# First products of the last two batches: two pairs of token blocks at once

## The chip, the cores and the metric

The kernel runs on one core of one Trainium2 chip. A core has a matrix engine (PE; PEld is its weight load), a vector engine (DVE), a scalar engine (ACT), a general one (POOL, also called GpSimd) and a queue engine that issues most transfers (SP). The metric is the device time of one execution in microseconds. Before the change the median of three runs is 464.58 us (464.53 to 464.72).

## The reference

Four batches of 768 tokens. An attention with a decaying state gives x with 384 columns (8 heads of 48), and a mixer follows:

```python
    for t in range(S):
        state = f[:, :, t, :, None] * state + np.einsum('bhd,bhe->bhde', k[:, :, t], v[:, :, t])
        y[:, :, t] = np.einsum('bhd,bhde->bhe', q[:, :, t], state)
...
    xt = x.transpose(0, 2, 1)
    h = xt @ U @ V
    u = x + h.transpose(0, 2, 1)
    ch = np.maximum(u @ w_ch1, 0.0) @ w_ch2
    return (u + ch).astype(np.float32)
```

`f` is the sigmoid of `f_logit`. `w_ch1` is 384x1536, `w_ch2` 1536x384; everything is float32.

## The kernel before

**Attention.** There are 16 units (4 batches by 4 pairs of heads). A unit's tokens are cut into 12 chunks; scans on DVE (L936, L954) give the decays, PE makes scores (`sc`, L1035), turns (`pt`), what a chunk adds to the state (`ds`, L1086) and the output (`y`, L1129 and L1147), all products on a part of the array. Between these stand pieces of the mixer of the batch before, as filler for PE.

**Mixer.** x of a batch lies as 6 blocks of 128 tokens. The low-rank part (`ph`, `pu`) is added to x; then pairs of blocks are turned (`put`, L327; copied to `uT` by ACT, L328), so that a batch has 3 pairs. *First products* give z, 1536 hidden columns for each token, and ReLU. For batches 0 and 1 they are plain (`pz`, L339): 128x128 weights by the 256 columns of a pair of blocks. *Second products* multiply z of a pair with w2 in 7 block products instead of 8 (`pw`, L428, 192 columns). For this each pair needs four ready sums S1 to S4 of 128x768 (`sums_of`): S1 = z10 + z11, S2 = S1 − z00, S3 = z00 − z10, S4 = z01 − S2, where z with index r, c is token block r and half c of the hidden columns. S1 and S2 feed products themselves.

**Batches 2 and 3.** Their six pairs (0 to 5) take the first products through `fewer(a)` (`pp`, L536). A pair is 2 token blocks by 3 blocks of x's columns, w1 3 by 3 blocks of 512 columns, and 15 products take the place of 18. They multiply sums of x (10 for each pair, `X_SUMS`, DVE) with sums of w1 (14, made once by `sum_of_w`, L989). Each is done in four column groups of 128x128 weights by 128 columns of x: 60 products for each pair, 360 in all. Two products share a tile of PSUM. `settle` then combines them by a list, `VALUES`: 21 operations of 512 columns on each pair (19 adds on DVE, 2 copies on ACT), and a ReLU by ACT (L526) where one of z's six blocks is complete.

**Order.** The pieces from the last attention steps to the end are not run when they are called but recorded; `ORDER2`, a list written out by hand (243 numbers before), sets the order in which they are issued. Each engine then works through its own instructions in that order and waits by semaphores for what it needs. PSUM has three buffers of two banks (`ps_big`: `pp`, `put`, `pu` and one `pw`) and two of one bank (`ps_mm`: `pz`, `pw` and others). `Fill` gives attention its filler: `kept` holds the second products of batch 1's last pair, which are left for it.

Of the kernel before, what the change touches and what calls it, by code (L numbers as in the profile page):

```python
# [194 lines left out]
class Mixer:  # L195
# [6 lines left out]
    def __init__(self, tc, b, x, U, V, w1, w2, sums, ident, blocks, out, two, three, zp, ps_big, ps_mm, wide=False,  # L202
                 z_all=None, room=None, pair=0, kept=0):
# [129 lines left out]
        def ch1(a, j):  # L333

            pm = ps_mm.tile([P, 512], F32, name="pz", tag="mm")
            for i in range(2):
                for m in range(NDC):
                    o = (2 * j + i) * P
                    nc.tensor.matmul(pm[:, i * 2 * P : (i + 1) * 2 * P], lhsT=w1[:, m, o : o + P],  # L339
                                     rhs=uT[a][:, m, :], start=(m == 0), stop=(m == NDC - 1))  # L340
# [77 lines left out]
        def products(a, parts, *of):  # L418

            if 0 in parts:  # L420
                if (room["last"] == a - pair) if room else (a == NA - 1 - kept):
                    W["pm"] = ps_big.tile([P, 2, 512], F32, name="pw", tag="big")[:, 0]
                else:
                    W["pm"] = ps_mm.tile([P, 512], F32, name="pw", tag="mm")
            for n in parts:
                lhs, rhs = of[n]
                for i in range(NI):
                    nc.tensor.matmul(W["pm"][:, n * HM : (n + 1) * HM], lhsT=lhs[:, i, :], rhs=rhs[:, i, :],  # L428
                                     start=(i == 0), stop=(i == NI - 1))
# [4 lines left out]
        def seven(a, step, parts=(0, 1)):  # L434
            x0, x1 = x_of.get(2 * a, x[:, 2 * a, :]), x_of.get(2 * a + 1, x[:, 2 * a + 1, :])
            last_of_all = b == out.shape[0] - 1 and a == NA - 1
            if step == 0:
# [8 lines left out]
            elif step == 1:  # L446
# [10 lines left out]
            elif step == 2:  # L457
# [3 lines left out]
                add(W["o1"], W["o1"], pm[:, 0:DM], ALU.add)  # L461
                store(2 * a + 1, W["o1"])
                add(W["s"][:, hi], W["s"][:, hi], pm[:, hi], ALU.add)
                if last_of_all:
                    store(2 * a, W["o0"], lo)
# [1302 lines left out]
```

## Time and profile before

| | before |
|---|---|
| median of 3 runs | 464.58 us |
| the profiled execution | 465.49 us |
| its span | 463.8 us |
| busy PE, DVE, ACT, POOL | 454.1, 363.0, 171.9, 49.5 us |
| PE on `pz`, `pw`, `pp` in the chain that ended last | 18%, 27%, 18% of the span |
| granted clock | 0.998 |

The span is the time from the first to the last instruction of the profiled execution. PE is busy to 98% of it; before about 170 us there are short gaps, later hardly any. A product in float32 shows as two instructions of PE.

### The profile page before, as it was taken

The page shows a single profiled execution, that of the slowest core. Times are in us where ns is not written, and L with a number is a line of the kernel's source. Part 1 is how long each engine was busy: PE and PEld are TensorE (multiplying, and loading weights), DVE is VectorE, ACT ScalarE, POOL GpSimd, SP SyncE. Part 2 cuts the span into 40 slices and gives each one's busy share as a digit, 9 for nine tenths or more (in the row PEclk, how much of TensorE's full clock was granted, in tenths as well). Part 3 has the DMA queues.
Part 4 walks back from the last instruction along what each step waited for, and adds up shares of the span by engine and source line. Part 5 has one row for each costly group of instructions (what it writes and reads, how often), then busy time and mean ns, then how long its engine had stood idle before and what let it go on. Part 6 is the DMA issues. An engine that isn't in the chain of part 4 may idle for free.

```text
span 463.8 us, 13155 instructions
## 1 busy us (share of the span) xinstructions
PE 454.1 (98%) x5687; PEld 394.9 (85%) x5687; DVE 363.0 (78%) x614; ACT 171.9 (37%) x325; POOL 49.5 (11%) x58
## 2 busy tenths in 40 slices
PE   8999999999999999999999999999999999999997
PEld 5876888876666578899988889999989999999996
DVE  6668688988999689677799895879797974878652
ACT  6765776644332135234413542241212311212200
POOL 2002345544110101011000000000000000000000
PEclk9999999999999999999999999999999999999999
DMA  9948997678778814662406100000000100000001
GB/s 193 191 106 211 228 205 175 157 132 111 111 113 120 127 21 55 90 90 28 86 1 112 29 3 11 29 1 1 17 19 1 36 0 18 18 1 35 1 35 40
DMA packets 148584, 34.37 MB, mean 74 GB/s; under 512 B 136934, under 2 KB 146982, under 8 KB 148518
## 3 DMA queue, kind: packets, MB, share of 16 engines
q1 hardware_dynamic: 147718, 33.29, 37.2%
q8 instruction: 47, 0.77, 0.7%
q10 hardware_dynamic: 800, 0.15, 0.2%
q14 instruction: 19, 0.16, 0.1%
HBM read 28.70 MB, written 4.72 MB: 72 GB/s over the span
## 4 chain that ended last, share of the span: by engine, by line
PE 84%; DVE 7%; SPq 2%; ACT 2%; issue 2%; DMA 2%; POOL 0%; DVEq 0%; ACTq 0%; POOLq 0%
PE pw L428 27%; PE pz L339 18%; PE pp L536 18%; PE po L394 5%; PE y L1129 2%; SPq L721 2%; PE sc L1035 2%; PE y L1147 2%; PE ds L1086 2%; PE pt L1062 1%; DVE late L936 1%; PE put L327 1%; PE pt L837 1%; PE pt L895 1%; DMA w<-in_q_dram 1%
## 5 line engine op out<-in xcount | busy, mean ns | idle before, releaser
L339 PE MATMUL pz<-uT,w 128*128 128x256 f32 x420 | 96.4, 383 | 0.1
L339 PEld LDWEIGHTS pz<-uT,w 128*128 128x128 f32 x420 | 77.9, 190 | 10.9 <-ACT uT L328 0.3
L428 PE MATMUL pw<-w,z_all 128*128 128x192 f32 x216 | 37.7, 328 | 0.0
L428 PE MATMUL pw<-zw,w_raw 128*128 128x192 f32 x216 | 37.6, 328 | 0.0
L428 PEld LDWEIGHTS pw<-w,z_all 128*128 128x128 f32 x216 | 35.1, 190 | 0.9 <-DVE qT L243 0.5
L428 PEld LDWEIGHTS pw<-zw,w_raw 128*128 128x128 f32 x216 | 35.2, 190 | 0.5 <-issue 0.3
L116 POOL TENSOR_TENSOR w<-w_y,w_r 128x384 int32<-128x384 int32 x24 | 31.5, 1312 | 36.9 <-DVE w_y L115 22.5
L526 ACT ACTIVATE other<-other 128x512 f32<-128x512 f32 x18 | 11.4, 631 | 44.2 <-DVE other L243 44.2
L526 ACT ACTIVATE z_all<-z_all 128x512 f32<-128x512 f32 x18 | 11.3, 630 | 40.4 <-DVE z_all L243 40.4
L936 DVE TENSOR_TENSOR_SCAN late<-fz,late 128x768 f32<-128x768 f32 x12 | 21.1, 1754 | 6.6 <-ACT fz L931 6.5
L374 ACT ACTIVATE z_all<-pz 128x512 f32<-128x512 f32 x27 | 16.1, 597 | 26.9 <-PE pz L339 26.5
L394 PE MATMUL po<-w,zw 128*128 128x384 f32 x72 | 25.1, 495 | 0.0
L394 PE MATMUL po<-w,z_all 128*128 128x384 f32 x72 | 24.7, 493 | 0.0
L536 PE MATMUL pp<-v_nat,late 128*128 128x128 f32 x168 | 21.6, 276 | 0.0
L394 PEld LDWEIGHTS po<-w,zw 128*128 128x128 f32 x72 | 13.2, 190 | 9.6 <-issue 0.8
L1117 POOL COPY st<-added 128x576 f32<-128x576 f32 x8 | 12.5, 1560 | 81.0 <-DVE added L1111 64.6
L954 DVE TENSOR_TENSOR_SCAN late<-fz,other 128x768 f32<-128x768 f32 x12 | 21.0, 1748 | 0.1
L394 PEld LDWEIGHTS po<-w,z_all 128*128 128x128 f32 x72 | 13.3, 190 | 8.9 <-DVE o L243 0.6
L536 PEld LDWEIGHTS pp<-v_nat,late 128*128 128x128 f32 x168 | 20.2, 192 | 0.1
L1094 ACT COPY added<-ds 48x576 f32<-48x576 f32 (+2 forms) x29 | 17.8, 619 | 5.8 <-PE ds L1086 5.4
L536 PE MATMUL pp<-uT,late 128*128 128x128 f32 x144 | 19.3, 277 | 0.0
L113 DVE TENSOR_SCALAR w_y<-w_y 128x384 f32<-128x384 f32 (+3 forms) x27 | 12.1, 448 | 8.9 <-ACT w_y L106 8.9
(219 smaller groups left out, 908.4 us busy)
## 6 DMA issues: line engine op xcount, KB each, us to landing
w_raw<-in_moe_w_ch_dram SPq DMA_DIRECT2D x18, 384.0 KB, 3.8
out_dram<-o SPq DMA_DIRECT2D x17, 192.0 KB, 1.9
v_nat<-in_v_dram SPq DMA_DIRECT2D x16, 144.0 KB, 3.5
v_nat<-in_v_dram SPq DMA_DIRECT2D x32, 72.0 KB, 3.6
zw<-in_moe_w_ch_dram SPq DMA_DIRECT2D x6, 384.0 KB, 4.5
out_dram<-o SPq DMA_DIRECT2D x14, 96.0 KB, 2.2
w<-in_k_dram SPq DMA_DIRECT2D x4, 288.0 KB, 3.9
w<-in_q_dram SPq DMA_DIRECT2D x4, 288.0 KB, 4.3
```

The source lines that it names most:

```text
L113: nc.vector.tensor_scalar(f, f, SMALLEST, LARGEST, ALU.max, ALU.min)
L116: nc.gpsimd.tensor_tensor(dst.bitcast(I32), shaped(y.bitcast(I32)), shaped(r), ALU.add)
L339: nc.tensor.matmul(pm[:, i * 2 * P : (i + 1) * 2 * P], lhsT=w1[:, m, o : o + P], rhs=uT[a][:, m, :], start=(m == 0), stop=(m == NDC - 1))
L374: nc.scalar.activation(z[a, c][:, k : k + 2, :].rearrange("p i t -> p (i t)"), pm, AF.Relu)
L394: nc.tensor.matmul(pm, lhsT=z[a, i // NI][:, i % NI, s * P : (s + 1) * P], rhs=w2[:, i, :], start=(i == 0), stop=(i == NFC - 1))
L428: nc.tensor.matmul(W["pm"][:, n * HM : (n + 1) * HM], lhsT=lhs[:, i, :], rhs=rhs[:, i, :], start=(i == 0), stop=(i == NI - 1))
L526: nc.scalar.activation(dst, dst, AF.Relu, scale=float(SIGNS[n]))
L536: nc.tensor.matmul(pm[:, i, r * P : (r + 1) * P], lhsT=room["w"](wn)[:, r * P : (r + 1) * P], rhs=x_node(a, xn), start=((xn, wn) == of[0]) ...
L936: nc.vector.tensor_tensor_scan(backwards(X, S - 1, S), backwards(f, S, S), backwards(ends, S - 1, S), 0.0, ALU.mult, ALU.add,)
L954: nc.vector.tensor_tensor_scan(Y, f[:, 0:S], starts, 0.0, ALU.mult, ALU.add)
L1094: nc.scalar.copy(added[r, 1:].rearrange("p (e c s) -> p e c s", c=NBL, s=2)[:, e], ds[r, :, 0 : NBL * D].rearrange("p s (c e) -> p e c s", ...
L1117: nc.gpsimd.tensor_copy(st, states.rearrange(by_e, c=NCH))
```

## The change

The six pairs are taken in three joints of two: 0 and 1, 2 and 3, 4 and 5. `joint(j, of)` replaces `fewer(a)`. A product takes the 256 columns of both pairs at once (block r of either pair, side by side), and the 15 products are gone through twice, once for each half c of z's columns. So there are 180 products of 256 columns, 30 sums of x of 256 columns, and as many operations of 512 columns behind the products as before. For a half to be a run of columns in each of w1's three blocks, w1's blocks of 128 columns are stored in another order (`AT`). `uT` gets four fixed slots in one tile, whose last is also `fz1` of the attention; the sums of x have one set of places, so that those of the next joint are made among the products of the second half. z lies in five thirds that go round, and three sums of w1 are copied to other places by ACT (`move_w`).

The ready sums are four pieces now (`sum_of`), and for pairs 1 and 3 S1 and S2 are made on GpSimd (`SUMS`), in all four operations of 128x768 there. `KEPT = 13` of 17 kept pieces stay in the attention; the others stand among the first joint's products. `ORDER2` is written anew, with 315 numbers.

Three places show the new order. First, PE from the last attention unit to the first `pp`, with tile names (`sc`, `ds`, `y` as above; `pw_3544`, `pw_3658`, `pw_3732` are the kept second products of batch 1). Before:

```order
L1086 MATMUL ds_3690<-v_nat_3422,kb_3654 48x48 x24
L428 MATMUL pw_3658<-zw_2308,w_raw_3534 128x192 x6
L428 MATMUL pw_3732<-w2_90,z_all_82 128x192 x6
L1035 MATMUL sc_3740<-qT_3552,kz1_131 64x64 x24
L1147 MATMUL y_3665<-v_nat_3301,A_3614 64x48 x24
L1129 MATMUL y_3791<-st_3717,qT_3552 64x48 x22
L428 MATMUL pw_3732<-zw_2306,w_raw_3532 128x192 x6
L536 MATMUL pp_3829<-uT_3205,late_80 128x128 x4
L536 MATMUL pp_3829<-v_nat_3563,late_80 128x128 x4
L1147 MATMUL y_3791<-v_nat_3422,A_3739 64x48 x24
```

and in the change:

```order
L1109 MATMUL ds_3653<-v_nat_3410,kb_3592 48x48 x24
L433 MATMUL pw_3596<-w2_90,z_all_82 128x192 x6
L1058 MATMUL sc_3698<-qT_3518,kz1_131 64x64 x24
L433 MATMUL pw_3724<-zw_2301,w_raw_3548 128x192 x6
L1152 MATMUL y_3731<-st_3682,qT_3518 64x48 x22
L1170 MATMUL y_3628<-v_nat_3074,A_3550 64x48 x24
L1170 MATMUL y_3731<-v_nat_3410,A_3697 64x48 x24
L1024 MATMUL pp_3811<-turns_128,late_80 128x256 x2
L1024 MATMUL pp_3811<-v_nat_3540,late_80 128x256 x2
```

Pieces of `pw` have left the last unit, and all of the last unit's `y` stands ahead of the first `pp`.

Second, PE from the end of joint 0 into the first half of joint 1, in the change (`pp_4045` is the last product of joint 0, the `pp` behind it belong to joint 1; `pw_4068` and `pw_4110` are second products of pair 0, and `w1_89` under `pw_4110` is its S2, which lies in a place of w1):

```order
L1024 MATMUL pp_4034<-v_nat_3544,late_80 128x256 x2
L1024 MATMUL pp_4045<-v_nat_3544,z_all_82 128x256 x2
L433 MATMUL pw_4068<-w2_90,other_81 128x192 x6
L1024 MATMUL pp_4075<-st_3541,late_80 128x256 x2
L1024 MATMUL pp_4075<-v_nat_3540,late_80 128x256 x2
L433 MATMUL pw_4068<-w2_90,z_all_82 128x192 x6
L1024 MATMUL pp_4091<-st_3541,w1_89 128x256 x2
L1024 MATMUL pp_4091<-turns_128,w1_89 128x256 x2
L1024 MATMUL pp_4096<-turns_128,late_80 128x256 x2
L1024 MATMUL pp_4096<-v_nat_3540,late_80 128x256 x2
L433 MATMUL pw_4110<-zw_2301,w1_89 128x192 x6
```

Between the last product of a joint and the first use of S2 stand two parts of `pw` and three pairs of products. Before, two pairs of blocks did not end together and each pair's sums were made apart.

Third, DVE at the same place. The last add behind `pp_4045`, then the five ready sums that are left to it (S1 of pair 0, S3 of pair 1, S2 of pair 0, S4 of pair 1, S4 of pair 0; S3 of pair 0 was made earlier), and what is queued behind:

```order
L959 TENSOR_TENSOR z_all<-z_all,pp 128x512
L247 TENSOR_TENSOR w_89<-other,z_all 128x768
L247 TENSOR_TENSOR w_raw<-other 128x768
L247 TENSOR_TENSOR w_89<-w_89,other 128x768
L247 TENSOR_TENSOR w_raw<-z_all,w_raw 128x768
L247 TENSOR_TENSOR w_89<-z_all,w_89 128x768
L247 TENSOR_TENSOR w_y<-x,pw 128x192
L247 TENSOR_TENSOR o<-w_y,pw 128x192
L959 TENSOR_TENSOR qT<-kz_131,pp 128x512
```

and POOL's whole list for the joints (S1 and S2 of pair 1, then of pair 3):

```order
L417 TENSOR_TENSOR w_raw<-other,z_all 128x768
L417 TENSOR_TENSOR w_raw<-w_raw,other 128x768
L417 TENSOR_TENSOR w_raw<-other,z_all 128x768
L417 TENSOR_TENSOR w_raw<-w_raw,z_all 128x768
L1767 TENSOR_LOAD ok
```

POOL's S1 waits for the same ReLU as DVE's S1, and DVE's S4 of pair 1 for POOL's S2.

The diff, cut to its core:

```diff
--- before.py
+++ after.py
 ORDER2 = (
-    1, 6, 0, 2, 3, 4, 47, 5, 8, 9, 10, 7, 11, 12, 13, 15, 14, 16, 18, 20, 17, 19, 21, 22, 61, 23, 26, 25, 27, 28,
...
+    10, 1, 2, 0, 3, 4, 5, 6, 8, 7, 9, 11, 12, 13, 14, 15, 16, 17, 18, 19, 20, 21, 22, 23, 25, 26, 27, 24, 28, 29,
...
-            uT[a] = three.tile([P, NDC, 2 * P], F32, name="uT")
+            uT[a] = three.tile([P, NDC, 2 * P], F32, name="uT") if uT_all is None else uT_all(b, a)
...
-                o = (2 * j + i) * P
+                o = at[2 * j + i] * P
...
-            return z[a, c][:, :, r * P : (r + 1) * P]
-
-        def sums_of(a):
-            for i in range(1, 5):
-                if room and a >= pair and (a - pair) % 2 == 0:
-                    s = room["S"][i - 1]
-                else:
-                    s = two.tile([P, WP], U64, name="w_raw", bufs=RAW).bitcast(F32)
-                S[a, i] = s.rearrange("p (i t) -> p i t", t=P)
-            add(S[a, 1], part(a, 1, 0), part(a, 1, 1), ALU.add)
-            add(S[a, 2], S[a, 1], part(a, 0, 0), ALU.subtract)
-            add(S[a, 3], part(a, 0, 0), part(a, 1, 0), ALU.subtract)
-            add(S[a, 4], part(a, 0, 1), S[a, 2], ALU.subtract)
+            return placed[a, r, c] if (a, r, c) in placed else z[a, c][:, :, r * P : (r + 1) * P]
+
+        def sum_of(a, i):
+            if room and a >= pair and (a - pair) % 2 == 0:
+                s = room["S"][i - 1]
+            else:
+                s = two.tile([P, WP], U64, name="w_raw", bufs=RAW).bitcast(F32)
+            S[a, i] = s.rearrange("p (i t) -> p i t", t=P)
+            left, right, op = {1: (part(a, 1, 0), part(a, 1, 1), ALU.add), 2: (S.get((a, 1)), part(a, 0, 0), ALU.subtract),
+                               3: (part(a, 0, 0), part(a, 1, 0), ALU.subtract), 4: (part(a, 0, 1), S.get((a, 2)), ALU.subtract)}[i]
+            if room and i in room["sums"](b, a):
+                nc.gpsimd.tensor_tensor(S[a, i], left, right, op)
+            else:
+                add(S[a, i], left, right, op)
...
-        def x_node(a, n):
-            if n < 6:
-                return uT[a][:, n % 3, n // 3 * P : (n // 3 + 1) * P]
-            return sums_x[a][n - 6]
...
-            def two_of(k):
-                if k == 0:
-                    free.extend(room["values"]())
-                    z[a, 0], z[a, 1] = zf[:, 0:NI, :], zf[:, NI:, :]
-                pm = ps_big.tile([P, 2, 512], F32, name="pp", tag="big")
-                for i, of in enumerate(PRODUCTS[k : k + 2]):
-                    for r in range(FG):
-                        for xn, wn in of:
-                            nc.tensor.matmul(
-                                pm[:, i, r * P : (r + 1) * P], lhsT=room["w"](wn)[:, r * P : (r + 1) * P],
-                                rhs=x_node(a, xn), start=((xn, wn) == of[0]), stop=((xn, wn) == of[-1]),
-                            )
-                    have[k + i] = pm[:, i, 0 : FG * P].rearrange("p (i t) -> p i t", t=P)
-                settle()
...
-            return [] if sums is None else [(1, lambda: sums_of(a))]
+            return [] if sums is None else [(1, lambda i=i: sum_of(a, i)) for i in range(1, 5)]
...
-    fz = [const.tile([P, S + 1], F32, name=f"fz{i}") for i in range(2)]
+    turns_of = const.tile([P, 4 * NDC * 2 * P + 1], F32, name="turns")
+    slots = turns_of[:, 0 : 4 * NDC * 2 * P].rearrange("p (n m t) -> p n m t", n=4, m=NDC)
+    fz = [const.tile([P, S + 1], F32, name="fz0"), turns_of[:, 3 * S :]]
+
+    def slot_of(b, a):
+        return slots[:, (a if b < B - 2 else a + (b - B + 2) * NBL // 2) % 4]
...
+    AT = [i % (NFC // 2) // 2 * 4 + 2 * (i // (NFC // 2)) + i % 2 for i in range(NFC)]
...
+            some = []
+            for i in range(3):
+                some.append(three.tile([P, NBL, 2, D], F32, name="v_nat").rearrange("p c h d -> p (c h d)"))
+                if i < 2:
+                    some.append(two.tile([P, NCH, D], F32, name="st").rearrange("p c d -> p (c d)"))
+            x_places.extend(t[:, i * 2 * P : (i + 1) * 2 * P].rearrange("p (s t) -> p s t", t=P) for t in some for i in range(2))
...
+    NI = NFC // 2
+    thirds = [t[:, i * NI : (i + 1) * NI, :] for t, n in ((of_other, 2), (z_all, 3)) for i in range(n)]
+    room["sums"] = lambda b, a: [(), (1, 2), (3,), (3, 4)][SUMS[(b - B + 2) * NBL // 2 + a]]
+    SUMS = 0, 1, 0, 1, 0, 0
+
+    def move_w(i):
+        t = late.rearrange("p a s -> p (a s)")[:, (4, 7)[i] * FG : ((4, 7)[i] + 1) * FG] if i < 2 else one.tile([P, 2, NBL, PAD], F32, name="kb").rearrange("p h c d -> p (h c d)")[:, 0:FG]
+        nc.scalar.copy(t, w_places[13 + i])
+        w_places[13 + i] = t
...
+    of_z = {}
+
+    def joint(j, of):
+
+        uT = slots[:, j % 2 * 2 : j % 2 * 2 + 2]
+        if j == 0:
+            of_z.update({(0, 0): 0, (0, 1): 1, (1, 0): 2, (1, 1): 3, "free": 4})
+        else:
+            of_z.update({(0, 0): of_z["free"], (1, 0): of_z[0, 0], (1, 1): of_z[1, 0], "free": of_z[1, 1]})
+        z = {cr: thirds[i] for cr, i in of_z.items() if cr != "free"}
+        for s, (m, a) in enumerate(of):
+            for (c, r), t in z.items():
+                m.placed[a, r, c] = t[:, :, s * P : (s + 1) * P]
+
+        def x_node(n):
+            if n < 6:
+                return uT[:, :, n % 3, n // 3 * P : (n // 3 + 1) * P]
+            return places_of_x()[[i for i, *_ in X_SUMS].index(n)]
+
+        def sum_of_x(i):
+            n, p, sign, q = X_SUMS[i]
+            combine(x_node(n), x_node(p), sign, x_node(q))
+
+        def half(c):
...
+            def two_of(k):
+                pm = ps_big.tile([P, 2, 512], F32, name="pp", tag="big")
+                for i, ((xn, wn),) in enumerate(PRODUCTS[k : k + 2]):
+                    for r in range(2):
+                        o = (2 * c + r) * P
+                        nc.tensor.matmul(
+                            pm[:, i, r * 2 * P : (r + 1) * 2 * P].rearrange("p (s t) -> p s t", t=P),
+                            lhsT=w_node(wn)[:, o : o + P], rhs=x_node(xn), start=True, stop=True,
+                        )
+                    have[k + i] = pm[:, i, :].rearrange("p (i t) -> p i t", t=2 * P)
+                settle()
+
+            return [(4 * 2 * P * len(PRODUCTS[k : k + 2]), lambda k=k: two_of(k)) for k in range(0, len(PRODUCTS), 2)]
+
+        return [(1, lambda i=i: sum_of_x(i)) for i in range(len(X_SUMS))], half(0), half(1)
...
+    KEPT = 13
+    attention(pieces, Fill(kept[:KEPT], 33))
...
+    joints = [joint(j, [(mixers[b], a) for b, a in pairs[2 * j : 2 * j + 2]]) for j in range(NP)]
...
+    def mixed(*lists):
+
+        lists, out = [list(t) for t in lists], []
+        while any(lists):
+            out += [t.pop(0) for t in lists if t]
+        return out
+
+    def sums_among(half, j):
+
+        if j >= NP:
+            return half
+        x, out = joints[j][0], []
+        ends = {1: (0, 1, 2), 3: (3, 4), 4: (5, 6), 5: (7,), 7: (8, 9)}
+        for k, p in enumerate(half):
+            out += [p] + [x[i] for i in ends.get(k, ())]
+        return out
+
+    moves = [(1, lambda i=i: move_w(i)) for i in range(3)]
+    x, h0, h1 = joints[0]
+    todo = list(x)
+    todo += mixed(h0, low[:1] + kept[KEPT : KEPT + 1] + low[1:2] + kept[KEPT + 1 : KEPT + 2] + mixers[1].mixes + low[3:4])
+    todo += m.before[-1:] + mixed(sums_among(h1, 1), kept[KEPT + 2 :])
+    todo += moves
+    for j in range(NP):
+        (m0, a0), (m1, a1) = [(mixers[b], a) for b, a in pairs[2 * j : 2 * j + 2]]
+        todo += m0.ready(a0) + m1.ready(a1)
+        A, E = m0.halved(a0), m1.halved(a1)
+        if j + 1 < NP:
+            x, h0, h1 = joints[j + 1]
+            todo += mixed(h0, A)
+            if j == 0:
+                todo += low[4:]
+            todo += E[:2] + mixed(sums_among(h1, j + 2), E[2:])
...
+            todo += A + E
```

More of the change, by code (lines that the diff above doesn't have):

```diff
@@ L202, in __init__ @@
     def __init__(self, tc, b, x, U, V, w1, w2, sums, ident, blocks, out, two, three, zp, ps_big, ps_mm, wide=False,
-                 z_all=None, room=None, pair=0, kept=0):
+                 z_all=None, room=None, pair=0, kept=0, uT_all=None, at=None):
         nc = tc.nc
@@ L440, in seven @@
                     return
-                s = W["s"] = two.tile([P, WP], U32, name="w_y").bitcast(F32)
-                o = W["o0"] = three.tile([P, DM], F32, name="o")
+                s = W[a, "s"] = two.tile([P, WP], U32, name="w_y").bitcast(F32)
+                o = W[a, "o0"] = three.tile([P, DM], F32, name="o")
                 nc.scalar.copy(s[:, hi], pm[:, lo])
@@ L460, in seven @@
                     return
[L461 to L463 removed]
+                add(W[a, "o1"], W[a, "o1"], pm[:, 0:DM], ALU.add)
+                store(2 * a + 1, W[a, "o1"])
+                add(W[a, "s"][:, hi], W[a, "s"][:, hi], pm[:, hi], ALU.add)
                 if last_of_all:
[L465 removed]
+                    store(2 * a, W[a, "o0"], lo)
@@ L545, in second @@
+                add(W[a, "o0"][:, hi], W[a, "s"][:, hi], pm[:, lo], ALU.add)
+                store(2 * a, W[a, "o0"], hi if last_of_all else slice(0, DM))
         def second(a):
@@ L587, in __init__ @@
         self.mixes = [(DM, mix_four), (DM, lambda: [mix(t) for t in range(NG, NCH)])]
-        self.first, self.second, self.ready, self.fewer, self.halved = first, second, ready, fewer, halved
-        self.sums_of_x = lambda a: [(1, lambda: sums_of_x(a))]
+        self.first, self.second, self.ready, self.halved, self.placed = first, second, ready, halved, placed
 def quarters(nc, pool, w2):
@@ new lines, in combine, with place_of, got, settle @@
+    def combine(dst, a, sign, b):
+        nc.vector.tensor_tensor(dst, a, b, ALU.add if sign == "+" else ALU.subtract)
+    of_z = {}
[17 more added lines that the diff above has]
+        def half(c):
+            have, todo, values, uses = {}, list(VALUES), {}, {}
+            for i, v in enumerate(VALUES):
+                for o in (v[1], v[3]):
+                    uses[o] = i
+            def place_of(n):
+                if n < 6:
+                    return z[c, n // 3][:, n % 3 * 2 : n % 3 * 2 + 2, :]
+                if n not in values:
+                    values[n] = places_of_values().pop(0)
+                return values[n].rearrange("p (i t) -> p i t", t=2 * P)
+            def got(o):
+                return have.get(int(o[1:])) if o[0] == "p" else place_of(int(o[1:]))
+            def settle():
+                while todo:
+                    n, p, sign, q = todo[0]
+                    if any(o is not None and got(o) is None for o in (p, q)):
+                        return
+                    todo.pop(0)
+                    i = len(VALUES) - len(todo) - 1
+                    left, right = got(p), None if q is None else got(q)
+                    dst = place_of(n)
+                    if q is None:
+                        nc.scalar.copy(dst, left)
+                    else:
+                        combine(dst, left, sign, right)
+                    for o in (p, q):
+                        if o is not None and o[0] == "v" and int(o[1:]) >= 6 and uses[o] == i and int(o[1:]) != n:
+                            v_places.append(values.pop(int(o[1:])))
+                    if n < 6 and not any(v[0] == n for v in todo):
+                        nc.scalar.activation(dst, dst, AF.Relu, scale=float(SIGNS[n]))
+            def two_of(k):
[11 more added lines that the diff above has]
+        return [(1, lambda i=i: sum_of_x(i)) for i in range(len(X_SUMS))], half(0), half(1)
@@ L1383, in factored_path @@
                     [(t, lambda i=i: sum_of_w(i)) for i, t in enumerate(turns, early_sums)])
-    attention(pieces, Fill(kept[:-1], 33))
+    KEPT = 13
+    attention(pieces, Fill(kept[:KEPT], 33))
     mixers = [m, mixer(B - 1)]
```

104 lines of the change are left out of this document (14 added, 90 removed), and 23 rows, old and new, of the table ORDER2.

## The prediction

> **What bounds the kernel now.** I read the page's busy row first, then the table of windows over the stage that changes, then the chain of waits.
>
> ```profile
> PE 454.1 (98%) x5687; PEld 394.9 (85%) x5687; DVE 363.0 (78%) x614; ACT 171.9 (37%) x325; POOL 49.5 (11%) x58
> ```
> ```profile
> 250.00:290.00 40.00, 40.00 (x816) 35.85 (x818) 31.72 (x53) 17.80 (x30) 0.00 (x0) 1.00 0.14 27
> 375.00:400.00 25.00, 25.00 (x188) 25.00 (x187) 15.36 (x31) 4.54 (x9) 0.00 (x0) 1.00 0.02 9
> 400.00:425.00 25.00, 25.00 (x194) 25.00 (x193) 19.86 (x34) 4.86 (x8) 0.00 (x0) 1.00 0.07 25
> 425.00:450.00 25.00, 25.00 (x178) 25.00 (x178) 17.28 (x30) 4.10 (x7) 0.00 (x0) 1.00 0.05 16
> ```
>
> The columns of a window are its bounds, its length, busy time (and instructions) of PE, PEld, DVE, ACT and POOL, the granted clock, the DMA share and GB/s. From 250 us on PE has no gap and the clock is 1.00; DVE is busy for 61 to 79% and POOL for nothing. A microsecond of PE work taken out of this stage is therefore one off the span as long as DVE keeps up, and every wait that PE is given is one on it. The chain of waits, whose rows are runs of work with start, length and count, has the prices:
>
> ```profile
> 58.31 5.18 PE pz L339 x24
> 69.99 2.59 PE pz L339 x12
> 73.10 2.79 PE pz L339 x12
> 296.50 5.36 PE pp L536 x48
> 311.71 3.77 PE pp L536 x32
> 319.39 3.57 PE pp L536 x32
> 349.17 0.52 PE put L327 x12
> 399.89 1.95 PE pw L428 x12
> 436.93 23.42 PE pw L428 x144
> 460.37 0.35 DVE o L243
> ```
>
> Every float32 product of the program shows as two instructions here. One instruction of 128 columns (pp) takes 5.36/48 = 111.6 ns, of 256 columns (pz) 5.18/24 = 215.8 ns, of 192 columns (pw) 1.95/12 = 162.5 ns. The first run behind a product on a part of the array costs 0.20 us more (3.77 against 3.57, 2.79 against 2.59).
>
> **The change, part by part.** *Products.* 360 products of 128 columns (720 instructions, 80.35 us) become 180 of 256 (360 instructions, 77.69 us): 2.66 us less. The new order has 55 passages from partial to full products where there were 56: 0.20 us less. Together −2.86 us. I price the new pp like pz, since both multiply a 128x128 block of weights by 256 columns of SBUF; the bounds are nothing (256 columns cost two of 128) and this.
>
> [...] The sum goes by the rows.
>
> *Three pieces of second products* (pw, 36 instructions, 5.85 us) leave the attention stage and stand behind the first pp. PE's sum stays; what covers the last attention unit gets thinner. In the window from 250 to 290 us DVE is busy for 31.72 us; with 5.85 us of PE work fewer that is 31.72/34.15 = 93%. It fits, so I take 0; the other bound is a third of the cover lost, 2 us.
>
> *x sums, copies, order of w1's columns.* 60 DVE sums of 128 columns become 30 of 256, and three ACT copies of 512 are new; ACT was under 20% busy in the last three windows. They lie beside PE, so nothing by themselves. What they do to DVE's lag comes next.
>
> *The end of a joint.* There DVE must finish the adds behind the products before the ready sums S1 to S4 (768 columns), and S2 feeds a second product. Prices on DVE, from its timeline (start, length):
>
> ```profile
> 371.56 0.28 DVE L243 TENSOR_TENSOR st<-uT,v_nat 128x128 f32<-128x128 f32 x1
> 371.76 0.68 DVE L243 TENSOR_TENSOR z_all<-qT,kz 128x512 f32<-128x512 f32 x1
> 372.36 0.28 DVE L243 TENSOR_TENSOR st<-uT,v_nat 128x128 f32<-128x128 f32 x1
> 372.56 0.68 DVE L243 TENSOR_TENSOR z_all<-z_all,pp 128x512 f32<-128x512 f32 x1
> 373.16 0.68 DVE L243 TENSOR_TENSOR qT<-pp,qT 128x512 f32<-128x512 f32 x1
> ...
> 396.06 0.96 DVE L243 TENSOR_TENSOR w_raw<-z_all 128x768 f32<-128x768 f32 x1 [0.49 <-ACT z_all L526]
> 397.06 0.96 DVE L243 TENSOR_TENSOR w_raw<-w_raw,z_all 128x768 f32<-128x768 f32 x1
> 397.93 0.95 DVE L243 TENSOR_TENSOR w_raw<-z_all 128x768 f32<-128x768 f32 x1
> ...
> 438.80 0.69 DVE L243 TENSOR_TENSOR z_all<-z_all,pp 128x512 f32<-128x512 f32 x1
> 440.18 0.96 DVE L243 TENSOR_TENSOR w_raw<-z_all 128x768 f32<-128x768 f32 x1 [0.70 <-ACT z_all L526]
> ```
>
> From start to start an add of 512 columns takes 0.60 us (a dependent one some 0.1 more, I use 0.62), a 128-column sum 0.20, so 256 columns about 0.34; a 768-column sum 0.87, or 1.00 ahead of one that needs it; and from the end of the last add through the ReLU to the first ready sum it is 0.70.
>
> Joint 0, second half, counted from the end of the first half's last product. PE: transposes 0.52, parts of pw 2.15 and 1.95, 13 products of 4 x 215.8 ns (11.22): the last product (the row pp_4045 in the excerpt) ends at 15.84. DVE has the first product of pp_3994 at about 8.3; from there it has 16 adds (9.9) and 6 x sums (2.0) without a gap, ends the last add at 20.2, and the ready sums can start at 20.9. PE goes on with pw 1.95, pp 1.73, pw 1.95, pp 1.73, pp 1.73 and wants S2 of the first pair (pw_4110) at 24.93: a slack of 4.0 us. In joint 1 the same count from the end of pp_4240 gives the last product at 22.70, the last add at 25.9, the sums from 26.6, and S2 wanted behind pw, pp, pp, pw (7.36) at 30.05: a slack of 3.5. On DVE alone S2 stands third, behind S1 of its own pair and S3 of the other: 0.87 + 0.96 + 0.96 = 2.8 us. Both fit, by 1.2 and 0.7 us.
>
> But the last ReLU releases POOL too, which makes S1 and then S2 of the other pair of each of these joints, as operations on two SBUF operands. POOL's prices by shape, from the groups of instructions:
>
> ```profile
> L116 POOL TENSOR_TENSOR U<-w_y,w_r 128x192 int32<-128x192 int32 x1 | 0.6, 593 | 29.5 <-DVE w_y L115 29.5
> L116 POOL TENSOR_TENSOR V<-w_y,w_r 128x128 int32<-128x128 int32 x1 | 0.5, 454 | 1.4 <-DVE w_y L115 1.4
> ```
>
> What the two engines do to each other, from the timeline of both:
>
> ```profile
> 64.82 1.75 DVE L936 TENSOR_TENSOR_SCAN late<-fz,late 128x768 f32<-128x768 f32 x1
> 65.05 2.32 POOL L116 TENSOR_TENSOR w<-w_y,w_r 128x384 int32<-128x384 int32 x1 [1.78 <-ACT w_y L106]
> ...
> 68.94 0.95 DVE L862 TENSOR_TENSOR kz<-pt,late 128x768 f32<-128x768 f32 x1
> 69.16 1.00 POOL L116 TENSOR_TENSOR w<-w_y,w_r 128x384 int32<-128x384 int32 x1 [1.79 <-DVE w_y L115]
> ...
> 71.29 1.75 DVE L954 TENSOR_TENSOR_SCAN late<-fz,other 128x768 f32<-128x768 f32 x1
> 71.52 2.31 POOL L116 TENSOR_TENSOR w<-w_y,w_r 128x384 int32<-128x384 int32 x1 [1.35 <-DVE w_y L115]
> 72.96 1.09 DVE L113 TENSOR_SCALAR w_y<-w_y 128x384 f32<-128x384 f32 x1
> ```
> ```profile
> 179.66 1.21 POOL L1117 COPY st<-added 128x576 f32<-128x576 f32 x1 [13.34 <-DVE added L1111]
> 180.43 1.26 DVE L865 TENSOR_TENSOR qT<-qT,late 128x768 f32<-128x768 f32 x1
> ```
>
> Beside a DVE operation with an operand in PSUM (pt, at 68.94) POOL's 384 columns take 1.00 us. Behind a scan with two SBUF operands the same takes 2.3: the scan ends at 66.57 and 73.04, POOL 0.80 later. In the other direction a 768-column DVE operation takes 1.26 instead of 0.95 behind POOL's copy, and the DVE operation that stood ready when the scan of 71.29 ended had to wait for POOL (to 74.05). So they take turns, whole operations at a time. POOL costs (1.00 − 0.454)/256 = 2.13 ns a column; 768 columns hold it for 0.80 + 0.82 = 1.62 us.
>
> Taken in turns S2 stands behind three DVE sums and two POOL sums: 2.8 + 2 x 1.62 = 6.1 us after the ReLU. PE then waits 6.1 − 4.0 = 2.1 us in joint 0 and 6.1 − 3.5 = 2.6 us in joint 1. Later waits there are covered: the buffer that the next but one pp wants (pp_4136) is free 9.9 us after the ReLU, and PE, held back already, comes for it at 11.8. The bounds of this term are 0 and, with a POOL sum at 2.0 us (POOL's 1.00 for 384 columns doubled, its start included), 2 x 0.4 more at each place, 6.3.
>
> [...]
>
> *The tail.* The last joint makes all its sums on DVE; its S2 (pair 4) is ready 5.95 to 6.5 us after the last product, by the same count, and wanted after 5.85 (three parts of pw): 0.1 to 0.7, I take 0.3. Behind it the tail is as before, pw and then the 0.35 us at 460.37 with its store.
>
> *Sum:* −2.86 + 2.1 + 2.6 + 0.3 = +2.1 us, 465.49 to 467.6 for the profiled execution. That one lies 0.91 us over the median and holds 463.8 us of span and 1.7 around it; the change leaves what is around, so the median goes from 464.58 to 466.7.
>
> **The rivals.** *No turns (sums on both engines side by side).* For it: none of the colliding rows above has float32 with two operands on POOL. Against it: all the colliding rows. It gives −2.86 + 0.3: 462.0. *DVE keeps its turn* through its three sums, since they stand back to back in its queue. For it: the next DVE sum is queued when one ends. Against it: 72.96, where the queued DVE operation lost. S2 then comes in time, but S4, which DVE makes next, waits for POOL's S2 at 6.1, and the evacuations behind it release a buffer late: about 0.5 us in joint 0 and 1.0 in joint 1, −1.1 in all: 463.5. *The attention stage runs dry* where the three pieces left: DVE ends it, 2 us on top of the forecast, 468.7, or about 464.0 with no turns. It decides from the point where DVE's 93% becomes 100. *Wide products cost two narrow ones:* the −2.66 is gone, 469.3; only a slower read of the two pairs' separate blocks could do it, and no row shows one.
>
> **How the numbers follow.** Forecast 0.47; no turns 0.25; DVE keeps its turn 0.13; attention dry 0.11; no gain of width 0.04. The 0.2% (0.93 us) that can be told from no change lies at 463.65 and 465.5. The forecast is slower except where slack or POOL's price are off by 1.2 us together (0.08 of its 0.47, same for most of that). No turns is faster but for 0.03; the third case is split between faster and same. Faster 0.32, same 0.16, slower 0.52. Range 461.8 to 468.6: from no turns without the tail's wait to the forecast with POOL near its upper bound.
>
> **What would show it.** Right: POOL's four sums of 128x768 at about twice their time beside a free DVE, or DVE's sums of 768 columns at about 2.5 us, two PE gaps of 2 to 3 us ahead of pw at the ends of joints 0 and 1, released by DVE's sum, and none in the attention stage. The new pp's at 216 ns an instruction. Wrong: PE without gaps there and DVE's sums at 0.95 us beside POOL's; or gaps in the last attention unit; or a pp of 256 columns at 223 ns.

## The result

| | before | the change |
|---|---|---|
| median | 464.53 us (9 runs, 463.59 to 465.59) | 468.22 us (9 runs, 465.83 to 469.22) |
| ratio, 95% interval | | 1.0076 [1.0057, 1.0096] |
| profiled execution, span | 465.49, 463.8 us | 469.22, 467.5 us |
| mean granted clock of that execution | 0.998 | 0.996 |

The change makes the kernel slower by 3.7 us. A second measurement gave 468.88 beside 464.75 us, ratio 1.0082 [1.0054, 1.0110]. The forecast was 466.7 us, slower, in a range of 461.8 to 468.6.

The page's busy row of the change, and the table of windows where the three pieces have left and at the program's start:

```profile
PE 453.5 (97%) x5327; PEld 383.1 (82%) x5327; DVE 364.1 (78%) x580; ACT 173.5 (37%) x328; POOL 60.6 (13%) x62
```
```profile
28.00:32.00 4.00, 4.00 (x67) 3.64 (x61) 1.36 (x1) 2.63 (x6) 0.00 (x0) 0.57 0.02 5
250.00:290.00 40.00, 39.91 (x847) 34.00 (x846) 32.09 (x51) 22.82 (x38) 0.00 (x0) 1.00 0.12 23
```

PE is busy for 0.6 us less than before, not 2.9, though it has 360 instructions fewer, and the span is 3.7 us longer. The view of waits names what PE waits for (engine, line, releaser, then the sum, how often, the longest):

```profile
PE pw L433 <- DVE w L247: 4.1, 3, 2.3
PE y L1170 <- issue: 1.6, 1, 1.6
```

The first row is new. The timeline at the end of joint 0 (start, length; all of DVE and POOL, and of the other engines only the ReLU and PE's pw) shows how it comes about:

```profile
328.46 0.63 ACT L1017 ACTIVATE z_all<-z_all 128x512 f32<-128x512 f32 x1 [0.90 <-DVE z_all L959]
329.12 0.96 DVE L247 TENSOR_TENSOR w<-other,z_all 128x768 f32<-128x768 f32 x1 [0.70 <-ACT z_all L1017]
329.17 2.58 POOL L417 TENSOR_TENSOR w_raw<-other,z_all 128x768 f32<-128x768 f32 x1 [110.65 <-ACT z_all L1017]
330.00 2.57 DVE L247 TENSOR_TENSOR w_raw<-other 128x768 f32<-128x768 f32 x1
331.83 2.41 POOL L417 TENSOR_TENSOR w_raw<-w_raw,other 128x768 f32<-128x768 f32 x1
332.49 2.56 DVE L247 TENSOR_TENSOR w<-w,other 128x768 f32<-128x768 f32 x1
334.97 0.95 DVE L247 TENSOR_TENSOR w_raw<-z_all,w_raw 128x768 f32<-128x768 f32 x1
335.10 2.22 PE L433 MATMUL pw<-zw,w 128*128 128x192 f32 x12 [1.68 <-DVE w L247]
```

S1 of pair 0 (DVE, 0.96), S1 of pair 1 (POOL, to 331.75), S3 (DVE, to 332.57), S2 of pair 1 (POOL, to 334.24), S2 of pair 0 (DVE, to 335.05): one at a time, each of the two DVE operations lengthened by the POOL sum ahead of it. The PE row stands in PE's own timeline: S2 is used 0.05 us after it is there, and PE had been idle for 1.68 us. Joint 1 reads alike (DVE's sums up to S2):

```profile
385.27 0.63 ACT L1017 ACTIVATE z_all<-z_all 128x512 f32<-128x512 f32 x1 [0.90 <-DVE z_all L959]
385.94 0.96 DVE L247 TENSOR_TENSOR w<-other,z_all 128x768 f32<-128x768 f32 x1 [0.70 <-ACT z_all L1017]
385.98 2.59 POOL L417 TENSOR_TENSOR w_raw<-other,z_all 128x768 f32<-128x768 f32 x1 [51.75 <-ACT z_all L1017]
386.81 2.57 DVE L247 TENSOR_TENSOR w_raw<-z_all,other 128x768 f32<-128x768 f32 x1
388.65 2.40 POOL L417 TENSOR_TENSOR w_raw<-w_raw,z_all 128x768 f32<-128x768 f32 x1
389.31 2.55 DVE L247 TENSOR_TENSOR w<-w,z_all 128x768 f32<-128x768 f32 x1
391.91 2.22 PE L433 MATMUL pw<-zw,w 128*128 128x192 f32 x12 [2.25 <-DVE w L247]
```

Rows of the change's chain of waits complete the account:

```profile
50.99 7.97 PE pz L343 x36
335.10 2.22 PE pw L433 x12
337.32 1.73 PE pp L1024 x8
339.05 1.95 PE pw L433 x12
391.91 2.22 PE pw L433 x12
440.38 23.68 PE pw L433 x144
```

and one of the chain before:

```profile
49.69 7.97 PE pz L339 x36
```

The first run of 36 pz starts at 50.99 us. The same run started at 49.69 before, so 1.3 us are lost at the program's start, where PE idles for 1.63 us at 25 us and the granted clock is then 0.57 from 28 to 32 us. The last pw take 23.68 us instead of 23.42, and the pw behind the two gaps take 2.22 instead of 1.95 (in the chain; a timeline shows 2.22 and 2.11, as runs overlap there): a run that starts behind a wait costs 0.27 us more, called a restart below. The sum for the profiled executions: −2.86 (products, passages) + 4.1 (gaps) + 0.8 (three restarts) + 1.3 (start) = +3.3 of the measured 3.7 us.

### The profile page after: what moved, and what is told of

Same layout as the page of the kernel before. It is cut to its first block, busy times and chain, and to the rows that moved or that the text cites. A ratio compares the mean times of both kernels' runs of the same rounds, so it can differ in the third digit from the quotient of the medians.

```text
span 467.5 us, 12433 instructions
## 1 busy us (share of the span) xinstructions
PE 453.5 (97%) x5327; PEld 383.1 (82%) x5327; DVE 364.1 (78%) x580; ACT 173.5 (37%) x328; POOL 60.6 (13%) x62
## 4 chain that ended last, share of the span: by engine, by line
PE 85%; DVE 9%; ACT 2%; issue 1%; DMA 1%; SPq 0%; DVEq 0%; ACTq 0%
PE pw L433 24%; PE pz L343 20%; PE pp L1024 13%; PE po L398 10%; PE sc L1058 3%; PE y L1152 2%; PE y L1170 2%; PE ds L1109 2%; DVE w L247 2%; PE pt L1085 2%; DVE z_all L959 2%; PE pt L832 1%; PE pt L774 1%; DVE w_raw L247 1%; PE put L331 1%
## 5 line engine op out<-in xcount | busy, mean ns | idle before, releaser
L343 PE MATMUL pz<-turns,w 128*128 128x256 f32 x420 | 96.2, 383 | 0.1
L343 PEld LDWEIGHTS pz<-turns,w 128*128 128x128 f32 x420 | 77.9, 190 | 10.9 <-ACT turns L332 0.3
L433 PE MATMUL pw<-w,z_all 128*128 128x192 f32 x252 | 44.3, 328 | 0.0
L433 PEld LDWEIGHTS pw<-w,z_all 128*128 128x128 f32 x252 | 41.5, 190 | 1.0
L417 POOL TENSOR_TENSOR w_raw<-other,z_all 128x768 f32<-128x768 f32 x2 | 5.2, 2584 | 162.4 <-ACT z_all L1017 162.4
L1024 PE MATMUL pp<-v_nat,late 128*128 128x256 f32 x104 | 26.2, 379 | 0.0
L1140 POOL COPY st<-added 128x576 f32<-128x576 f32 x8 | 13.6, 1704 | 81.7 <-DVE added L1134 81.7
L433 PE MATMUL pw<-zw,w 128*128 128x192 f32 x108 | 19.2, 329 | 4.1 <-DVE w L247 4.1
L433 PEld LDWEIGHTS pw<-zw,w 128*128 128x128 f32 x108 | 17.7, 190 | 5.3 <-DVE w L247 5.1
```

Of the source, the lines that this page charges most:

```text
L433: nc.tensor.matmul(W[a, "pm"][:, n * HM : (n + 1) * HM], lhsT=lhs[:, i, :], rhs=rhs[:, i, :], start=(i == 0), stop=(i == NI - 1))
L1024: nc.tensor.matmul(pm[:, i, r * 2 * P : (r + 1) * 2 * P].rearrange("p (s t) -> p s t", t=P), lhsT=w_node(wn)[:, o : o + P], rhs=x_node(xn) ...
L1140: nc.gpsimd.tensor_copy(st, states.rearrange(by_e, c=NCH))
```

## The experiments

The theory was the one of the forecast: at a joint's end POOL's and DVE's sums take turns, and S2 comes late. The first rival was that DVE is late there whoever helps it; the order, the moved pieces and the width of the products stood to be separated from both.

### No sum on POOL

```diff
-    SUMS = 0, 1, 0, 1, 0, 0
+    SUMS = 0, 0, 0, 0, 0, 0
```

> The change, with SUMS all 0: DVE makes the four sums that POOL made; nothing is left out. On DVE S2 of the first pair stays third in line (S1 of either pair ahead of it). Turns theory: DVE's sums go back from 2.49 to 0.96 us, S2 is ready 2.8 us after the ReLU, the PE gaps of 1.7 and 2.2 us ahead of pw and the 0.27 us of restart behind each are gone: 4.4 us faster than the change, about 463.8 us. Rival, DVE is late at a joint's end whoever helps it: two more sums for DVE at each of the two joints (4 x 0.87 us), so no faster than the change, 468 to 471 us.

Measured: 462.66 us (10 runs, 461.76 to 463.40), ratio to the kernel before 0.9939 [0.9915, 0.9963]. The timeline of this kernel at the same place:

```profile
327.79 0.96 DVE L247 TENSOR_TENSOR w<-other,z_all 128x768 f32<-128x768 f32 x1 [0.70 <-ACT z_all L1017]
328.67 0.95 DVE L247 TENSOR_TENSOR w_raw<-other,z_all 128x768 f32<-128x768 f32 x1
329.54 0.95 DVE L247 TENSOR_TENSOR w<-w,other 128x768 f32<-128x768 f32 x1
...
331.92 2.11 PE L433 MATMUL pw<-zw,w 128*128 128x192 f32 x12
```

Seven sums stand in a row (the first three are shown) at 0.87 us from start to start; S2, the third of them, is there at 330.5, and PE comes for it at 331.92 without a wait. With more to do DVE is in time, so the rival falls: it was not too slow, it was held up. This kernel beats both: 2.4 us less than the kernel before on that chip (465.03), and 5.6 and 6.2 us less than the two medians of the change. A gain of at least 5.6 against an expected 4.4 was the first sign that the gaps cost more than their own length.

### One turn in the line instead of two

```diff
-    room["sums"] = lambda b, a: [(), (1, 2), (3,), (3, 4)][SUMS[(b - B + 2) * NBL // 2 + a]]
+    room["sums"] = lambda b, a: [(), (1,), (3,), (3, 4)][SUMS[(b - B + 2) * NBL // 2 + a]]
```

> The change, with only S1 of pairs 1 and 3 on POOL, S2 of these pairs on DVE, where it stands between S1 and S2 of the first pair; nothing is left out. Turns theory: one POOL sum stands in the line instead of two, S2 is ready at 3 x 0.93 + 1.62 = 4.4 us after the ReLU instead of 6.0; gaps of about 0.3 and 0.8 us and their restarts are left, so 2.8 us faster than the change, about 465.4 us. Rival, DVE is late anyway: one more DVE sum a joint, slower than the change, 468 to 470 us.

Measured: 464.26 us (10 runs), ratio to before 0.9977 [0.9956, 0.9998], 1.6 us over the kernel with no sum on POOL. PE's gap in its timeline at joint 0, and then at joint 1:

```profile
332.76 2.22 PE L433 MATMUL pw<-zw,w 128*128 128x192 f32 x12 [0.24 <-DVE w L247]
...
388.14 2.22 PE L433 MATMUL pw<-zw,w 128*128 128x192 f32 x12 [0.83 <-DVE w L247]
```

0.24 and 0.83 us, where 0.3 and 0.8 were expected. DVE is late for another reason than in the change, though, as the timeline of DVE and POOL at joint 0 shows:

```profile
328.22 0.96 DVE L247 TENSOR_TENSOR w<-other,z_all 128x768 f32<-128x768 f32 x1 [0.69 <-ACT z_all L1017]
328.26 2.58 POOL L417 TENSOR_TENSOR w_raw<-other,z_all 128x768 f32<-128x768 f32 x1 [110.65 <-ACT z_all L1017]
330.88 0.96 DVE L247 TENSOR_TENSOR w_raw<-w_raw,other 128x768 f32<-128x768 f32 x1 [1.70 <-POOL w_raw L417]
331.76 0.95 DVE L247 TENSOR_TENSOR w<-w,other 128x768 f32<-128x768 f32 x1
```

DVE's second sum is now S2 of pair 1, which needs the S1 that POOL makes. DVE waits 1.70 us for these data, and S2 of pair 0 stands behind it in DVE's queue. So this kernel shows what one POOL sum in the line costs, but not that the engines take turns. It helps in another way: with DVE idle, POOL's sum ends 1.66 us after DVE's S1 (330.84 after 329.18); in the change, with a DVE sum held up beside it, 1.67 us after (331.75 after 330.08). The held sum did not slow POOL, so the two did not share; one waited.

### POOL's sum away from the joint's end

```diff
-    SUMS = 0, 1, 0, 1, 0, 0
+    SUMS = 0, 2, 0, 2, 0, 0
```

> The change, with S3 of pairs 1 and 3 on POOL in place of S1 and S2; nothing is left out. S3 needs only the first half of z, so POOL can make it in the middle of the second half, far from the line of the joint's end. Turns theory: POOL's sum takes 1.6 to 2.6 us and holds up one or two DVE adds by up to 0.8 us there, which DVE's lag passes on to the ReLU (slack 4.0 and 3.5 against 2.8); gaps of 0 to 0.3 us, so within 0.5 us of the kernel with no sum on POOL, about 463.9 us. Rival, any POOL sum between the joints costs its length: half of what the change lost, about 466 us.

Measured: 462.74 us (12 runs), ratio to before 0.9949 [0.9929, 0.9968]: as with no sum on POOL. DVE and POOL in the timeline around POOL's second S3:

```profile
365.81 0.69 DVE L959 TENSOR_TENSOR qT<-A,kz 128x512 f32<-128x512 f32 x1
365.93 2.25 POOL L417 TENSOR_TENSOR w_raw<-z_all,other 128x768 f32<-128x768 f32 x1 [54.21 <-DVE st L959]
366.41 0.55 DVE L247 TENSOR_TENSOR o<-o,pw 128x384 f32<-128x384 f32 x1
366.88 0.35 DVE L247 TENSOR_TENSOR w_y<-w_y,pw 128x192 f32<-128x192 f32 x1
```

POOL waits for DVE's add of two SBUF operands (to 366.50) and then holds on for 1.68 us; DVE's next two operations, which read pw from PSUM, run beside it at 0.55 and 0.35 us, as in the kernel with no sum on POOL. So it is not a sum on POOL that costs, but one whose turn falls between sums of two SBUF operands that PE waits for. It gained nothing either. Of the DVE operations of these rows and of joint 0 that stood beside a float32 sum on POOL, those with two SBUF operands took turns with it (2.57 and 2.56 us behind it in joint 0 instead of 0.95), and the two with an operand in PSUM kept their 0.55 and 0.35 us.

### The width alone

```diff
-                        nc.tensor.matmul(
-                            pm[:, i, r * 2 * P : (r + 1) * 2 * P].rearrange("p (s t) -> p s t", t=P),
-                            lhsT=w_node(wn)[:, o : o + P], rhs=x_node(xn), start=True, stop=True,
-                        )
+                        for s in range(2):
+                            nc.tensor.matmul(
+                                pm[:, i, (2 * r + s) * P : (2 * r + s + 1) * P],
+                                lhsT=w_node(wn)[:, o : o + P], rhs=x_node(xn)[:, s, :], start=True, stop=True,
+                            )
```

beside `SUMS = 0, 0, 0, 0, 0, 0`.

> As the kernel with no sum on POOL, and each product of 256 columns made as two of 128 with the same weights block; nothing is left out. If width is worth what the rows of pz and pp said, 360 more instructions cost 2.66 us more: 466.4 us, less what the slower PE hides of waits (under 0.3). If width were worth nothing the time stays as with 256 columns.

Measured: 465.18 us (11 runs, 464.00 to 466.50; a twelfth took 473.35 us at a mean clock of 0.982), ratio to before 0.9997 [0.9976, 1.0018]. It is 2.5 us over the same kernel with 256 columns. The expectation's 466.4 stood on a base of 463.8; on the measured base of 462.66 it would have been 465.3. So the width is worth what pz and pp of the kernel before said. Order, moves and places without it come to nothing together: this kernel takes the time of the kernel before, within 0.24%.

### The change once more

> The change once more, unaltered, beside the runs of the kernel before on the same chip. The two PE gaps with their restarts (1.68 + 2.25 + 0.18 us and 3 x 0.27 us) less the 2.86 us of products make +2.1 us; the profiled execution of the change also had a stretch from 28 to 32 us at a granted clock of 0.57, about 1.3 us. If that stretch is not of the change, it comes and goes, and the median lies about 2.1 to 2.5 us over the kernel before, or 4.7 us over the kernel with no sum on POOL (467.2 beside 465.0). If it belongs to the change, it is 3.4 to 3.7 us again.

Measured: 468.88 us (7 runs, 466.33 to 470.96), 4.1 us over before. Neither case of the expectation fits: the slow start is not in this profile, and the loss is there. The table of windows of this execution, and PE's timeline behind joint 1's gap:

```profile
389.00:391.00 2.00, 0.52 (x3) 0.52 (x4) 2.00 (x2) 0.00 (x0) 0.61 (x1) 0.99 0.00 0
391.00:393.00 2.00, 2.00 (x8) 2.00 (x7) 2.00 (x5) 0.00 (x0) 0.00 (x0) 0.50 0.01 4
393.00:395.00 2.00, 2.00 (x8) 1.89 (x8) 2.00 (x5) 0.00 (x0) 0.00 (x0) 0.65 0.00 0
395.00:397.00 2.00, 2.00 (x13) 1.87 (x12) 1.54 (x4) 0.00 (x0) 0.00 (x0) 1.00 0.00 0
```
```profile
390.48 3.77 PE L433 MATMUL pw<-zw,w 128*128 128x192 f32 x12 [2.25 <-DVE w L247]
394.04 1.21 PE L1024 MATMUL pp<-v_nat,fz 128*128 128x256 f32 x4
```

Behind the same gap of 2.25 us the granted clock is 0.50 and 0.65 for 4 us, and 12 pw take 3.77 us where 2.22 stood in the first profile of the change. 4 us at a mean of 0.58 are 1.7 us lost. So the low clock is not of the start alone: here it follows a gap that the change made. On this chip 5 of 7 executions of the change have a mean clock of 0.996 or less, and none of 12 of the kernel before. (One stretch as this, 1.7 us lost of 465, makes a mean of 0.996.) Both measurements of the change together: in 6 of 16 executions the mean clock is over 0.996, and their median is 466.8 us (465.83 to 467.84), 2.1 us over the same kind of execution of the kernel before (464.7); in the other 10 the median is 469.05 us, 2.3 us more.

### A third place with turns

```diff
-    SUMS = 0, 1, 0, 1, 0, 0
+    SUMS = 0, 1, 0, 1, 0, 1
```

> The change, with S1 and S2 of pair 5 on POOL too, as those of pairs 1 and 3; nothing is left out. Turns theory: at the last joint's end S2 of pair 4 has no slack (PE waits 0.18 us there already) and then stands behind two POOL sums more, 2 x 1.62 us: a third PE gap of 3.4 us in place of 0.2, so 3.2 us slower than the change, about 470.5 to 471.5 us. Rival, the gaps come from something else than POOL's sums at a joint's end (DVE's load, the new order): DVE has two sums less there, so the same as the change or up to 0.5 us faster.

Measured: 471.48 us (6 runs), ratio to before 1.0136 [1.0116, 1.0157]; 3.3 us over the first measurement of the change, 2.6 over the second, which was taken on the same chip. PE's gap in the last joint:

```profile
443.17 4.17 PE L433 MATMUL pw<-zw,w 128*128 128x192 f32 x24 [3.40 <-DVE w L247]
```

3.40 us where the change waits for 0.18: 3.22 us more, two POOL sums of 1.61 us. Taking two sums off DVE made it later. In this profile too the clock drops behind joint 1's gap of 2.25 us (0.77, 0.50 and 0.88 in the windows of 2 us from 389 to 395 us); behind the gap of 3.40 us it does not (1.00 from 443 to 451 us).

### The gaps filled, and one gap at a time

In the first of three kernels PE works on in the gaps, to see whether the low clock comes without the pause:

```diff
+            if room and 0 in parts and (a, 2) in S and of[0][0] is S[a, 2]:
+                for _ in range({0: 5, 2: 6}.get((b - 2) * 3 + a, 0)):
+                    nc.tensor.matmul(W[a, "pm"][:, 0:HM], lhsT=w2[:, 0, 0:P], rhs=w2[:, 0, 0:HM], start=True, stop=True)
             for n in parts:
                 lhs, rhs = of[n]
```

> The change, with PE kept at work in the two gaps: 5 and 6 products of 192 columns on weights that are long loaded (1.63 and 1.95 us) stand ahead of the pw that waits; their results are overwritten by that pw, and nothing is left out. PE waits for S2 as before, so the gaps stay in the schedule. Clock theory (a PE gap of 1.7 to 2.3 us is at times followed by some 3.5 us at half the granted clock, 1.8 us lost and more): no such stretch behind the joints any more, and no restart of 0.27 us, so the executions lie where those of the change without a stretch lie, 465.8 to 466.5 us, against 468.9 for the median of the change on the same kind of run. Rival, the low clock comes with the program's start or the chip and not with the gaps: 468 to 469 us as the change.

Measured: 467.49 us (13 runs, 466.29 to 470.12), ratio to before 1.0039 [1.0014, 1.0064]. A low mean clock is left in 1 of 13 executions (0.993, 470.12 us). That one is the profiled one. There PE's clock is 1.00 behind both joints, and the first of two slow stretches stands near the program's start, again behind a gap of 1.6 us:

```profile
PE y L1173 <- issue: 1.6, 1, 1.6
```
```profile
28.00:30.00 2.00, 2.00 (x12) 2.00 (x11) 1.24 (x1) 1.21 (x4) 0.00 (x0) 0.55 0.06 18
30.00:32.00 2.00, 2.00 (x53) 1.70 (x52) 0.12 (x1) 1.19 (x2) 0.00 (x0) 0.60 0.00 0
34.00:40.00 6.00, 5.37 (x200) 4.26 (x201) 4.76 (x12) 4.44 (x14) 1.05 (x2) 1.00 0.58 162
40.00:100.00 60.00, 59.54 (x502) 49.74 (x503) 50.98 (x91) 38.23 (x76) 27.96 (x22) 0.97 0.82 190
336.00:340.00 4.00, 3.98 (x22) 3.78 (x23) 3.93 (x7) 0.00 (x0) 0.00 (x0) 1.00 0.00 0
392.00:394.00 2.00, 1.69 (x11) 1.39 (x10) 2.00 (x3) 0.00 (x0) 0.00 (x0) 1.00 0.02 4
394.00:396.00 2.00, 2.00 (x13) 1.87 (x12) 2.00 (x5) 0.00 (x0) 0.00 (x0) 1.00 0.00 0
```

The second lies between 40 and 100 us, where a mean clock of 0.97 is 1.8 us lost. PE is idle for 0.63 us from 34 to 40 us and for 0.46 us in those 60, 1.09 us in all, less than the one gap of 1.6 us ahead of the first: a pause as long as that is not always what comes before a drop. That the low clock is gone behind the joints, and with it most of the slow executions, bears the clock theory out, although the median is 1 us above the band expected. Against the 466.8 us of the change's own undisturbed clock it is 0.6 to 0.7 us, and what that is made of stays open. In this profile PE still waits for 0.32 us behind the fill of joint 1 and the pw behind both fills still take 2.22 us.

The other two have the turns in one joint only:

```diff
-    SUMS = 0, 1, 0, 1, 0, 0
+    SUMS = 0, 0, 0, 1, 0, 0
```

> The change, with S1 and S2 on POOL for pair 3 only, so that joint 1 alone has the turns; nothing is left out. Turns theory: one PE gap of 2.25 us and its restart of 0.27 us, so 2.5 us over the kernel with no sum on POOL, 465.2 us where the clock stays at 1.00, and two more where it drops behind the gap; median 465 to 467.3 us, the mean clock 1.00 in the one kind and 0.996 in the other. Rival, both joints' turns are needed for the loss: as with no sum on POOL, 462.7 us.

Measured: 466.16 us (12 runs), ratio to before 1.0021 [0.9989, 1.0054]. The 7 executions at full clock have a median of 465.2 us, as expected. In 5 of 12 the mean clock is 0.996 or less (466.1 to 471.4 us), and the table of windows of the profiled one shows it behind the gap of 2.25 us again:

```profile
386.00:388.00 2.00, 0.33 (x2) 0.33 (x3) 2.00 (x2) 0.00 (x0) 0.81 (x1) 1.00 0.00 0
388.00:390.00 2.00, 2.00 (x10) 2.00 (x9) 2.00 (x4) 0.00 (x0) 0.00 (x0) 0.65 0.01 4
390.00:392.00 2.00, 2.00 (x7) 1.82 (x6) 2.00 (x5) 0.00 (x0) 0.00 (x0) 0.50 0.00 0
392.00:394.00 2.00, 2.00 (x12) 1.82 (x12) 1.55 (x4) 0.00 (x0) 0.00 (x0) 1.00 0.00 0
```

```diff
-    SUMS = 0, 1, 0, 1, 0, 0
+    SUMS = 0, 1, 0, 0, 0, 0
```

> The change, with S1 and S2 on POOL for pair 1 only; nothing is left out. Turns theory: one PE gap of 1.68 us and its restart, 1.95 us over the kernel with no sum on POOL, 464.6 us. Clock theory: the shorter gap is followed by a low clock more rarely than joint 1's, so the median stays within 0.5 us of 464.6 us. If a drop needs no more than a gap of 1.3 us it comes as often as in joint 1 and the median is 465 to 466.5 us.

Measured: 464.56 us (12 runs), ratio to before 0.9978 [0.9951, 1.0005]; 464.6 was expected. The gap is 1.68 us, and the mean clock is low in 1 of 12 executions. So joint 0 costs its own length and restart. Joint 1 costs that, and its kernel has a low mean clock in 5 of 12 executions; with so few of each, that 2.25 us draws more drops than 1.68 us is likely and not shown. How often the mean clock is low, by kernel:

| kernel | PE gaps at the ends of joints 0, 1 and 2, us | executions with a mean clock of 0.996 or less |
|---|---|---|
| before | no joints, no such gap | 10 of 74 |
| no sum on POOL; S3 on POOL | none, none, 0.2 | 0 of 22 |
| no sum on POOL, 128 columns | none | 1 of 12 |
| one turn | 0.24, 0.83, 0.2 | 1 of 10 |
| pair 1 only | 1.68, none, 0.2 | 1 of 12 |
| pair 3 only | none, 2.25, 0.2 | 5 of 12 |
| the change, both measurements | 1.68, 2.25, 0.18 | 10 of 16 |
| three places | 1.68, 2.25, 3.40 | 3 of 6 |
| the change, gaps filled | as the change, PE at work in the first two | 1 of 13 |

A mean does not say where in the program the clock was low. Of the profiles with a low mean, the first of the change, the one with one turn and the one with filled gaps have a stretch near the start (0.57 from 28 to 32 us, 0.66 from 24 to 28, 0.55 and 0.60 from 28 to 32); the second of the change, three places and pair 3 only have it behind joint 1's gap.

## Why the prediction came out as it did

*Products.* −2.66 was forecast, 2.5 measured by width alone. Eight instructions of 256 columns take 1.73 us, 216 ns each.

*Three pieces out of the attention stage.* 0 was forecast. PE is busy for 39.91 of the 40 us from 250 to 290 us while DVE has 32.09: no dry stage. This rival falls.

*Turns at the ends of joints 0 and 1.* 2.1 and 2.6 us were forecast, and 1.68 and 2.25 measured, each with a restart of 0.27 that the sum didn't have: 1.95 and 2.52. S2 came 5.96 us after the ReLU instead of 6.1 (the forecast's own terms, 2.8 + 2 x 1.62, make 6.04). POOL lengthened each of the two DVE sums behind it by 1.62 us, as worked out from its narrower operations. The slack was larger than forecast: PE stood idle from 4.33 us after the ReLU in joint 0 and from 3.76 in joint 1, not from 4.0 and 3.5. The rival without turns falls by the same rows; its 462.0 us is near the 462.66 of the kernel with no sum on POOL, where there is nobody to take turns with. The rival in which DVE keeps its turn falls by the order of the rows at 330.00 to 332.49.

*The tail.* 0.3 was forecast, 0.18 and a restart of 0.26 measured.

*What the sum lacked* is a size, not the mechanism. The executions at full clock have a median of 466.8 us, and 466.7 was forecast. That they meet so closely is luck: the three waits were forecast at 5.0 us and measured at 4.1, and restarts of 0.8 us, which the sum did not have, fill the difference. The term that was too small is the price of the gap: "PE then waits 6.1 − 4.0 = 2.1 us in joint 0 and 6.1 − 3.5 = 2.6 us in joint 1" took a wait for its length. Behind joint 1's gap the granted clock drops in three of the four profiles that have this gap unfilled, which costs 1.7 us each time, and executions with a low clock moved the median from +2.1 to +3.7 and +4.1 us. The trace of before held no price for it: its PE waits for 1.1 us at most at a time, so its clock of 1.00 was no promise for a kernel with longer gaps. That the median of 468.22 lies inside the range is luck too: the upper end of 468.6 was meant for a POOL sum near 2.0 us, and that sum took 1.62. The second measurement's 468.88 lies above it.

## What to carry over

Do not give a second engine a sum whose turn falls between two DVE operations that read SBUF twice and that somebody waits for (two such sums made PE wait for 1.68 and 2.25 us here); put it beside operations that read PSUM, or earlier, as S3 here, where it at least cost nothing. Where a matrix engine has been busy throughout, price a new gap with its restart (0.27 us here) and with a slow stretch behind it (1.7 us here; the mean clock was low in 5 of 12 to 10 of 16 executions of the kernels with a gap of 2.25 us, and in 1 of 12 of the kernel with 1.68 us alone), and look for the second in the mean clock of every execution, not of the one that was profiled.

## What the hardware did that was not expected

Pauses of 1.3 to 2.25 us were followed by a slow stretch of about 4 us (a mean granted clock of 0.57 from 28 to 32 us in the first profile of the change, of 0.58 from 391 to 395 us in the second), in some executions and not in others: 2.25 us in joint 1 with a clock of 1.00 behind it in the first profile of the change and 0.50 in the second, and 3.40 us in the last joint of the kernel with three places and no drop behind it. The drop stood behind 2.25 us in three profiles of four, behind pauses of 1.63, 1.6 and 1.28 us near the program's start in one profile each, and once, in the kernel with filled gaps, where PE's idle time from 34 us on was 1.09 us at most in all. The kernel with the 1.68 us of joint 0 alone had a low mean clock in 1 of 12 executions. What decides between two executions with the same gap no run here shows.
